# Layer 2's factor products with the weights stationary and 512 tokens moving, and finished tiles turned in 32x32 blocks for the stores

## The chip, the core and the metric

The kernel runs on one core of a Trainium2 chip. The metric is the device time of one execution in microseconds (us). Three runs of the kernel before gave 1584.54, 1584.80 and 1585.04 us; the median is 1584.8 us.

The core's engines are TensorE (PE in the profile, with its weight loads as PEld), VectorE (DVE), ScalarE (ACT), GpSimd (POOL) and SyncE (SP), which here issues nearly all DMAs. They run beside each other and wait for each other by semaphores.

## The reference

Linear attention per batch and head, an RMS norm, and then two feed-forward layers over 4608 tokens (512 wide, 2048 inside), all in float32:

```python
kv = np.einsum('bhsd,bhse->bhde', k, v)
out = np.einsum('bhsd,bhde->bhse', q, kv)
x = out / np.sqrt(np.mean(out * out, -1, keepdims=True) + 1e-6) * g_norm     # -> (4608, 512)
h = x @ w_in1;  x = (h * sigmoid(1.702 * h)) @ w_out1                         # layer 1
h = x @ w_in2;  y = (s * relu(h) ** 2 + b) @ w_out2                           # layer 2, the output
```

## The kernel before

**Numbers.** Every matrix product is made of three matmuls: each operand is split into a high part of reduced precision (fp32r) and a low part, and high x high, low x high and high x low are summed in PSUM.

**Stages.** Attention and the first three blocks of 512 tokens of layer 1 come first. The other six blocks of layer 1 run as three couples of two blocks, and the first eight blocks of layer 2 as four couples. In a couple the input product is made by Strassen-like seven products instead of eight (`product`, three matmuls for each of two 128-row halves, so six matmuls of 128 rows by 512 tokens). The last block of layer 2 is computed plainly (`last_mm1`, `last_mm2`) and is called the tail here.

**Ticks.** One `product` and what stands beside it is a tick; a couple has 8 x 7 = 56 ticks. Layer 2's couples begin at ticks 168, 224, 280 and 336, the tail at tick 392.

**Layer 2's output product.** It is done by seven factor products too. Two pairs of hidden blocks (14 ticks) make a quad. `factor_add` forms the seven sums of activations (names M1, M4, M7, M5, M6, M2, M3 in their order), `factor_hi` and `factor_lo` split each into two tiles `fac`. Factors take two pairs of places by turns: the one the places `wc` and `wo5`, the other `wo6` and `wo7`, so every second factor uses `wc`/`wo5`. `load_t` brings the factors of the weights from DRAM into a ring of five places. In each tick `quad_unit` computes one half (h = 0 or 1) of one factor: with 4 quads in each of 4 couples that is 4 x 4 x 7 x 2 = 224 units. A unit is 12 matmuls (lines 993 to 995): 128 tokens of `fac` are the stationary side, 256 columns of the weights move, and the result has tokens on the partitions. Five of the seven factors are drained by VectorE into an SBUF tile `madd` after each unit, from two PSUM banks taken by turns; M2 and M3 stay in PSUM over the whole couple (`msum`).

**Places in SBUF.** `PLACES` lays all tiles out one behind the other. Six small tiles of 32 bytes (`ms0 r0 ms1 r1 r2 r3`) stand behind `wf0`; all places named after them lie 192 bytes off the 2 KB grid of those named before (`kv`, `f`, `q`, `wraw`, `wst0`, `wc`, `xn`). `wo0` to `wo7`, `wi`, `xh`, `xl` and `wst1` are among the later ones.

**End of a couple.** `combine(s, h)`, once for each h, adds the seven factors on VectorE (line 89 records all VectorE and ScalarE work) and sends four results of 256 tokens x 256 columns each straight from `madd` with one DMA each on SP (line 1018).

**What sets the order.** The program order of each engine is written out: the loop over pairs and products calls `product`, `after`, `factors`, `beside_quads` and then `background`, which steps waiting tasks by release and due ticks. SP takes its DMAs strictly in that order: a DMA that waits for a tile holds all those behind it.

Of the kernel before, what the change touches and what calls it, by code (L numbers as in the profile page):

```python
# [16 lines left out]
P = 128  # L17
# [5 lines left out]
BT = 512  # L23
# [7 lines left out]
PARTS = HEAD + [(ALONE, 0, KF)]  # L31
SIZES = {"kv": 1024, "wraw": 1024, "wst": 1024, "wc": 1024, "wo": 1024, "f": 1024, "xh": 2048, "xl": 2048, "wi": 2048, "ms": H, "r": H}
PLACES = (
# [3 lines left out]
)  # L37
# [3 lines left out]
KP = DM // 2  # L41
# [11 lines left out]
def tile_attn_moe_moe2(  # L53
# [18 lines left out]
    nc = tc.nc  # L72
# [20 lines left out]
    vector = Metered(nc.vector, "dve", 75, 1.04)  # L93
    scalar = Metered(nc.scalar, "act", 95, 0.83)
# [32 lines left out]
    def bank(tag, name, shape=(P, BT)):  # L127
        return ps.tile(list(shape), F32, tag=tag, name=name)
# [550 lines left out]
    g2_t, c_t, ps_t, sums = {}, {}, {}, {}  # L679
# [291 lines left out]
    def held(q_, k_):  # L971
        return k_ in (M2, M3)

    def quad_unit(q_, k_, h):

        s, x = quads[q_]
        first, last = x == 0, x == KF // 2 // BY - 1
        hi, lo, _ = f_t[q_, k_]
        w = t_t[q_, k_]
        key = (s, k_, h)  # L980
        if not held(q_, k_):
            turns["m"] = turns.get("m", -1) + 1
            o = bank(("h1", "a1")[turns["m"] % 2], "m", (P, 2, KP))
        elif first:
            o = m_ps[key] = bank(f"y{len([0 for z in m_ps if z[0] == s])}", "msum", (P, 2, KP))
        else:
            o = m_ps[key]
        for c in range(2):
            cs = slice((2 * h + c) * P, (2 * h + c + 1) * P)
            for y in range(BY):  # L990
                begins = c == 0 and y == 0 and (first or not held(q_, k_))
                ends = c == 1 and y == BY - 1 and (last or not held(q_, k_))
                nc.tensor.matmul(o[:, c, :], hi[:, y, cs], w[:, y, 0, :], start=begins, stop=False)  # L993
                nc.tensor.matmul(o[:, c, :], hi[:, y, cs], w[:, y, 1, :], start=False, stop=False)  # L994
                nc.tensor.matmul(o[:, c, :], lo[:, y, cs], w[:, y, 0, :], start=False, stop=ends)  # L995
        if not held(q_, k_):
            if first:
                a = m_sb[key] = new(ADD_PLACE[10 + h if k_ == M1 and s % 2 else 2 * k_ + h], (P, 2, KP), name="madd")
                scalar.copy(a, o)
            else:  # L1000
                a = m_sb[key]
                vector.tensor_tensor(out=a, in0=o, in1=a, op=ALU.add)
        if last:
            ended.add(key)
        if h == 1:
            load_t()

    ended = set()

    def combine(s, h):  # L1010

        js, m = couples[s][2], couples[s][1]
        q_ = quads.index((s, 0))
# [6 lines left out]
        def plus(k_, more):  # L1020
            a = m_sb[s, k_, h]
            vector.tensor_tensor(out=a, in0=more, in1=a, op=ALU.add)

        def until(k_):
            while (s, k_, h) not in ended:
                yield 1

        sums = ((M7, M6), (M6, M5), (M5, M7), (M7, M4))
        plus(M6, m_sb[s, M1, h])
        if s == LAST - 1:  # L1030
            yield from until(M2)
            plus(M1, m_ps[s, M2, h])
            yield from until(M3)
            last = new(f"f{h}", (P, 2, KP), name="m3")
            scalar.copy(last, m_ps[s, M3, h])
            yield 4
            send(M1, 0, 0)
            for k_, e in sums:
                plus(k_, m_sb[s, e, h])
                yield 2  # L1040
            send(M5, 1, 1)
            plus(M6, last)
            yield 2
            send(M7, 1, 0)
            yield 2
            send(M6, 0, 1)
            return
        yield from until(M6)
        for k_, e in sums:
            plus(k_, m_sb[s, e, h])  # L1050
            yield 1
        send(M5, 1, 1)
        yield from until(M2)
        plus(M1, m_ps[s, M2, h])
        yield 1
        send(M7, 1, 0)
        yield 1
        send(M1, 0, 0)
        yield from until(M3)
        plus(M6, m_ps[s, M3, h])  # L1060
        yield 1
        send(M6, 0, 1)

    wo2_next = [0]

# [48 lines left out]
    n0 = begin[1, CUTS[-2]]  # L1114
# [10 lines left out]
    n0 = begin[ALONE, 0]  # L1125
# [85 lines left out]
    class Task:  # L1211
# [4 lines left out]
        def step(self, tick):  # L1216
            wait = next(self.gen, self)
            if wait is self:
                self.done = True
                tasks.remove(self)  # L1220
            else:
                self.ready = max(self.ready, tick + (wait or 0))

    def plan():

        n = KF // 2 * 7
        split = {}
        for s_ in range(len(couples)):
            n0 = n * s_
            need = []  # L1230
            if s_:
                if couples[s_][0]:
                    need = [Task(y_get(s_), n0 - n + 6, n0 - n + 7)]
                if s_ < LAST:
                    need = [Task(fac_sums(s_), n0 - (14 if s_ <= first2 else 35), n0 - 9, need)]
            for i in range(7 if s_ < LAST else 2):
                if (s_, i) in split_early:
                    continue
                more = [split[s_, 1]] if (i == 6 and s_ <= first2 and (s_, 1) in split) else []
# [19 lines left out]
    with tc.manual_schedule():  # L1259
# [10 lines left out]
        o = bank("h1", "warm")  # L1270
# [399 lines left out]
```

## Time and profile before

| what | value |
|---|---|
| median of three runs | 1584.8 us |
| the profiled execution's own time | 1585.22 us |
| its span, first to last instruction | 1583.5 us |
| TensorE matmuls in it | 8880, busy 99% of the span |
| VectorE, ScalarE busy | 63%, 59% |
| stores of layer 2's couples (line 1018) | 32 DMAs of 256 KB |

A busy TensorE is not TensorE at its peak: the profile's matmuls overlap, so what a matmul costs is read from the start of one to the start of the next, which the timeline shows. The profiled execution's span leaves 1.7 us of its time outside.

### The profile page before, as it was taken

What the parts mean: (1) busy time and instruction counts of PE and PEld (TensorE: products, weight loads), DVE (VectorE), ACT (ScalarE), POOL (GpSimd) and SP (SyncE); (2) the same over time, 40 slices, a digit from 0 to 9 for tenths busy, and PEclk for the clock granted to TensorE, in tenths of its full rate; (3) what the DMA queues carried; (4) which work ended last, traced back from release to release, by engine and by line L of the source; (5) the groups of instructions that cost most, each with busy time, mean ns of one, the idle gap of its engine ahead of it and who ended that gap; (6) DMA issues with size and microseconds to landing.
All of it is one profiled execution on the core that took longest, in us unless ns stands there. A gap on an engine that the chain in (4) does not pass through costs nothing.

```text
span 1583.5 us, 23132 instructions
## 1 busy us (share of the span) xinstructions
PE 1563.4 (99%) x8880; PEld 1338.7 (85%) x8880; DVE 1001.3 (63%) x1478; ACT 937.4 (59%) x1520; POOL 69.3 (4%) x49
## 2 busy tenths in 40 slices
PE   7999999999999999999999999999999999999999
PEld 6788888878887888888888899899999998999987
DVE  6877743456666666777885466866686668556620
ACT  4766643454445555464446866776677677766652
POOL 4000111101000010000000000000000000000000
PEclk9999999999999999999999999999999999999999
DMA  8678877567776876789975755685568556755563
GB/s 279 199 265 308 274 259 258 199 207 244 272 240 231 293 255 219 248 278 362 357 282 199 253 188 186 213 268 189 185 216 263 188 188 210 241 193 184 189 219 113
DMA packets 127039, 372.71 MB, mean 235 GB/s; under 512 B 12626, under 2 KB 29266, under 8 KB 119762
## 3 DMA queue, kind: packets, MB, share of 16 engines
q1 hardware_dynamic: 126786, 371.12, 69.6%
q8 instruction: 70, 1.15, 0.3%
q14 instruction: 39, 0.32, 0.1%
q10 hardware_dynamic: 144, 0.13, 0.0%
HBM read 289.41 MB, written 81.79 MB: 234 GB/s over the span
## 4 chain that ended last, share of the span: by engine, by line
PE 90%; DVE 5%; ACT 2%; DMA 2%; issue 1%; SPq 0%; POOL 0%; DVEq 0%; ACTq 0%; POOLq 0%
PE A L696 6%; PE A L697 6%; PE A L698 6%; PE m L995 4%; PE m L994 4%; PE m L993 4%; PE D L696 3%; PE D L697 3%; PE D L698 3%; PE sum L830 3%; PE sum L832 3%; PE sum L831 3%; PE acc L624 3%; PE acc L625 3%; PE z L830 3%; PE acc L626 3%
## 5 line engine op out<-in xcount | busy, mean ns | idle before, releaser
L995 PE MATMUL m<-wo,fac 128*128 128x256 f32 x640 | 180.8, 283 | 0.6 <-DVE fac L89 0.6
L994 PE MATMUL m<-wo,fac 128*128 128x256 f32 x640 | 180.7, 282 | 0.0
L993 PE MATMUL m<-wo,fac 128*128 128x256 f32 x640 | 180.0, 281 | 0.0
L89 ACT ACTIVATE gh<-gh 128x512 f32<-128x512 f32 x72 | 45.4, 632 | 145.3 <-DVE gh L89 145.2
L994 PEld LDWEIGHTS m<-wo,fac 128*128 128x128 f32 x640 | 122.2, 191 | 6.1
L993 PEld LDWEIGHTS m<-wo,fac 128*128 128x128 f32 x640 | 121.2, 189 | 7.0
L995 PEld LDWEIGHTS m<-wo,fac 128*128 128x128 f32 x640 | 121.2, 189 | 1.2 <-DVE fac L89 1.2
L696 PE MATMUL A<-wi,xl 128*128 128x512 f32 x296 | 117.5, 397 | 1.9 <-ACT ev L89 0.7
L697 PE MATMUL A<-wi,xl 128*128 128x512 f32 x296 | 116.2, 393 | 0.0
L698 PE MATMUL A<-wi,xl 128*128 128x512 f32 x296 | 115.2, 389 | 0.0
L89 DVE TENSOR_TENSOR madd<-m,madd 128x512 f32<-128x512 f32 x122 | 83.8, 688 | 49.4 <-PE m L995 49.4
L89 ACT ACTIVATE wraw<-wraw 128x512 uint32<-128x512 uint32 (+1 forms) x128 | 82.7, 646 | 52.6 <-DVE wraw L89 52.6
L425 POOL TENSOR_TENSOR r<-ms,mhalf 128x8 f32<-128x8 f32 x36 | 65.6, 1826 | 544.0 <-DVE ms L89 543.9
L89 DVE TENSOR_TENSOR fac<-s,fac 128x1024 fp32r<-128x1024 f32 x64 | 77.9, 1218 | 15.0 <-ACT fac L89 15.0
L89 ACT ACTIVATE g<-h 128x512 f32<-128x512 f32 x52 | 31.0, 597 | 79.8 <-PE h L598 69.6
L596 PE MATMUL h<-xh,wi 128*128 128x512 f32 x192 | 76.5, 399 | 1.2 <-ACT g L89 1.2
L830 PE MATMUL z<-wo,wo 128*128 128x512 f32 x192 | 76.1, 396 | 1.2 <-DVE g L89 0.7
L624 PE MATMUL acc<-gh,wo 128*128 128x512 f32 x192 | 76.7, 399 | 0.0
L625 PE MATMUL acc<-gh,wo 128*128 128x512 f32 x192 | 75.1, 391 | 0.7 <-DVE wo L89 0.7
L626 PE MATMUL acc<-gl,wo 128*128 128x512 f32 x192 | 75.0, 390 | 0.0
L598 PE MATMUL h<-xl,wi 128*128 128x512 f32 x192 | 74.9, 390 | 0.0
L832 PE MATMUL z<-wo,wo 128*128 128x512 f32 x192 | 74.9, 390 | 0.0
(264 smaller groups left out, 4370.7 us busy)
## 6 DMA issues: line engine op xcount, KB each, us to landing
wo<-wt SPq DMA_DIRECT2D x127, 512.0 KB, 4.0
wo<-wo SPq DMA_DIRECT2D x80, 512.0 KB, 5.1
xl<-wi SPq DMA_DIRECT2D x37, 1024.0 KB, 6.5
xl<-wi SPq DMA_DIRECT2D x37, 768.0 KB, 5.9
wi<-wst SPq DMA_DIRECT2D x40, 512.0 KB, 4.5
xh<-wi SPq DMA_DIRECT2D x19, 1024.0 KB, 6.7
wraw<-in_w_in SPq DMA_DIRECT2D x32, 512.0 KB, 4.1
wraw<-in_w_out SPq DMA_DIRECT2D x32, 512.0 KB, 4.4
```

Of the source, the lines that this page charges most:

```text
L89: return fn(*args, **kw)
L624: nc.tensor.matmul(o, wh[:, ds_], gh, start=(f == lo), stop=False)
L625: nc.tensor.matmul(o, wl[:, ds_], gh, start=False, stop=False)
L626: nc.tensor.matmul(o, wh[:, ds_], gl, start=False, stop=(f == hi - 1))
L696: nc.tensor.matmul(o, wh, xh, start=(c == 0 and not more), stop=False, skip_group_check=more)
L697: nc.tensor.matmul(o, wl, xh, start=False, stop=False, skip_group_check=more)
L698: nc.tensor.matmul(o, wh, xl, start=False, stop=(c == 1), skip_group_check=more)
L830: nc.tensor.matmul(o, wh[:, cs], gh, start=begins, stop=False)
L832: nc.tensor.matmul(o, wh[:, cs], gl, start=False, stop=ends)
L993: nc.tensor.matmul(o[:, c, :], hi[:, y, cs], w[:, y, 0, :], start=begins, stop=False)
L994: nc.tensor.matmul(o[:, c, :], hi[:, y, cs], w[:, y, 1, :], start=False, stop=False)
L995: nc.tensor.matmul(o[:, c, :], lo[:, y, cs], w[:, y, 0, :], start=False, stop=ends)
```

## The change

The operands of `quad_unit` change sides. The weights' factor (128 x 128) is the stationary side and all 512 tokens of `fac` move, so a unit is 6 matmuls of 512 columns (lines 992 to 994 of the new file), and the result has 128 output columns on the partitions and 512 tokens along the row. h now picks 128 of the 256 columns instead of 256 of the 512 tokens.

The output must have tokens as rows. So `combine`, now one task for both h, lets VectorE transpose each finished 128 x 512 tile in 32 x 32 blocks into one of three places, and four DMAs per tile put the blocks where they belong, in runs of 32 floats (128 bytes). The sums come in another order, and the sends have due ticks of their own (`COMBINE_DUE`, `LAST_DUE`, tables of due ticks counted from the couple's end). A 2 KB place `tr0` is added.

```diff
-    "kv0 kv1 f0 f1 f2 f3 f4 f5 q0 q1 wraw0 wraw1 wst0 wc xn0 xn1 wf0 "
+    "kv0 kv1 f0 f1 f2 f3 f4 f5 q0 q1 wraw0 wraw1 wst0 wc xn0 xn1 wf0 tr0 "
...
-        for c in range(2):
-            cs = slice((2 * h + c) * P, (2 * h + c + 1) * P)
-            for y in range(BY):
-                begins = c == 0 and y == 0 and (first or not held(q_, k_))
-                ends = c == 1 and y == BY - 1 and (last or not held(q_, k_))
-                nc.tensor.matmul(o[:, c, :], hi[:, y, cs], w[:, y, 0, :], start=begins, stop=False)
-                nc.tensor.matmul(o[:, c, :], hi[:, y, cs], w[:, y, 1, :], start=False, stop=False)
-                nc.tensor.matmul(o[:, c, :], lo[:, y, cs], w[:, y, 0, :], start=False, stop=ends)
+        hs = slice(h * P, (h + 1) * P)
+        for y in range(BY):
+            begins = y == 0 and (first or not held(q_, k_))
+            ends = y == BY - 1 and (last or not held(q_, k_))
+            nc.tensor.matmul(o, w[:, y, 0, hs], hi[:, y, :], start=begins, stop=False)
+            nc.tensor.matmul(o, w[:, y, 1, hs], hi[:, y, :], start=False, stop=False)
+            nc.tensor.matmul(o, w[:, y, 0, hs], lo[:, y, :], start=False, stop=ends)
...
-    def combine(s, h):
+    combined = {}
+
+    def combine(s):
+
+        js = couples[s][2]
+        last = s == LAST - 1
-        def send(k_, t, right):
-            row = js[0] * BT + t * m + 2 * h * P
-            dst = out[row:row + 2 * P, right * KP:(right + 1) * KP].rearrange("(c p) d -> p c d", p=P)
-            nc.sync.dma_start(out=dst, in_=m_sb[s, k_, h])
+        def send(k_, t, right, h):
+            row, col = js[t] * BT, (2 * right + h) * P
+            turns["z"] = turns.get("z", -1) + 1
+            z = new(("tr0", "kv0", "kv1")[turns["z"] % 3] if last else ("tr0", "ev0", "g1")[turns["z"] % 3], name="turned")
+            vector.transpose(out=z, in_=m_sb[s, k_, h])
+            dst = out[row:row + BT, col:col + P].rearrange("(b i) (a j) -> a i b j", i=32, j=32)
+            for a in range(P // 32):
+                nc.sync.dma_start(out=dst[a], in_=z[32 * a:32 * a + 32, :].rearrange("i (b j) -> i b j", j=32))
...
+        yield from until(M6)
+        for k_, e in ((M7, M6), (M6, M5), (M5, M7), (M7, M4)):
+            for h in range(2):
+                plus(k_, h, m_sb[s, e, h])
+                yield step()
+        if not last:
+            yield from until(M2)
+            for h in range(2):
+                plus(M1, h, m_ps[s, M2, h])
+                yield step()
+        for h in range(2):
+            send(M7, 1, 0, h)
+            yield step(1)
...
+    COMBINE_DUE = (6, 7, 10, 10, 11, 11, 12, 12, 13, 13, 13, 14, 15, 16, 17, 18, 18, 19, 19, 20, 21, 22, 23)
...
-                for h in range(2):
-                    Task(combine(s_, h), n0 + n + 2 + h, n0 + n + 7 + h)
+                combined[s_] = 0
+                Task(combine(s_), n0 + n + 2, lambda s_=s_, t=n0 + n: t + (LAST_DUE if s_ == LAST - 1 else COMBINE_DUE)[combined[s_]])
```

Where this moves instructions is seen on VectorE and SP behind the end of a couple. VectorE's program order there in the kernel before, from the product B of one pair to the product D; `madd` are the factors' sums, `msum` PSUM, `s1` to `s3` and `fac` the next quad's factors, `wi7`, `xh0`, `wraw` and `wst0` activations:

```order
L89 TENSOR_TENSOR wi7_9549<-B_9576,wi7_9549 128x512
L89 TENSOR_TENSOR fac_9554<-wraw1_9234,fac_9553 128x1024
L89 TENSOR_TENSOR madd_8258<-msum_8353,madd_8258 128x512
L89 TENSOR_TENSOR s1_9614<-wst0_9202,wraw1_9234 128x1024
L89 TENSOR_TENSOR fac_9617<-s3_9551,fac_9616 128x1024
L89 TENSOR_TENSOR wi7_9549<-A_9542,wi7_9549 128x512
L89 TENSOR_TENSOR s2_9673<-s1_9614,wraw0_9138 128x1024
L89 TENSOR_TENSOR xh0_9612<-D_9637,xh0_9612 128x512
```

The same stretch of VectorE's order in the changed kernel, where `turned` is the place that a transposed tile goes to:

```order
L89 TENSOR_TENSOR wi7_9210<-B_9229,wi7_9210 128x512
L89 TENSOR_TENSOR fac_9215<-wraw1_8965,fac_9214 128x1024
L89 STREAM_TRANSPOSE turned_9250<-madd_8086 128x512
L89 TENSOR_TENSOR s1_9264<-wst0_8939,wraw1_8965 128x1024
L89 STREAM_TRANSPOSE turned_9280<-madd_8106 128x512
L89 TENSOR_TENSOR fac_9267<-s3_9212,fac_9266 128x1024
L89 STREAM_TRANSPOSE turned_9306<-madd_8129 128x512
L89 TENSOR_TENSOR wi7_9210<-A_9203,wi7_9210 128x512
L89 TENSOR_TENSOR s2_9322<-s1_9264,wraw0_8887 128x1024
L89 STREAM_TRANSPOSE turned_9336<-madd_8151 128x512
L89 TENSOR_TENSOR xh0_9262<-D_9286,xh0_9262 128x512
```

Of the eight transposes of a couple four stand in this stretch and four behind it, one in each tick from 15 to 22 after the couple's end; before, the last addition of the couple stood here, and no result was sent after tick 16.

SP's program order behind the end of the first couple of layer 2 in the kernel before; `out<-madd` are the stores, `wo<-wt` and `xl<-wi` loads of weights, `f3<-y5` a load of the next couple's input:

```order
L1018 DMA out<-madd_8170 128x2x256
L498 DMA f3_9341<-y5_87 128x2x512
L125 DMA wo2_9535<-wt0_3842 128x1024
L1018 DMA out<-madd_8115 128x2x256
L1018 DMA out<-madd_8198 128x2x256
L125 DMA xl1_9540<-wi1_3_5356 128x2048
L1018 DMA out<-madd_8002 128x2x256
L1018 DMA out<-madd_8141 128x2x256
L125 DMA wo3_9601<-wt0_3842 128x1024
```

And in the changed kernel, where each tile's store is four DMAs `out<-turned` (the `x4` of a row):

```order
L1023 DMA out<-turned_9250 32x16x32 x4
L1023 DMA out<-turned_9280 32x16x32 x4
L125 DMA wo4_9304<-wt0_3843 128x1024
L1023 DMA out<-turned_9306 32x16x32 x4
L125 DMA xl0_9312<-wi1_3_5357 128x1536
L1023 DMA out<-turned_9336 32x16x32 x4
L125 DMA wo0_9362<-wt1_3844 128x1024
L1023 DMA out<-turned_9366 32x16x32 x4
L1023 DMA out<-turned_9393 32x16x32 x4
L125 DMA xh1_9399<-wi1_4_5897 128x2048
```

The stores of a couple are 32 DMAs of 64 KB instead of 8 of 256 KB, they begin three ticks later, and four or eight of them stand ahead of each weight load on the same queue.

## Rows read from the trace of the kernel before

**Rows 1.** The page: engines, granted TensorE clock by slice, the chain that ended last
```profile
PE 1563.4 (99%) x8880; PEld 1338.7 (85%) x8880; DVE 1001.3 (63%) x1478; ACT 937.4 (59%) x1520; POOL 69.3 (4%) x49
...
PEclk9999999999999999999999999999999999999999
...
PE 90%; DVE 5%; ACT 2%; DMA 2%; issue 1%; SPq 0%; POOL 0%; DVEq 0%; ACTq 0%; POOLq 0%
```

**Rows 2.** PE's groups by line and shape: xcount | busy us, mean ns | idle
```profile
L995 PE MATMUL m<-wo,fac 128*128 128x256 f32 x640 | 180.8, 283 | 0.6 <-DVE fac L89 0.6
...
L995 PE MATMUL msum<-wo,fac 128*128 128x256 f32 x256 | 72.2, 282 | 0.0
```

**Rows 3.** Timeline of PE (start us, us): first factor matmul, first matmul after the last
```profile
880.53 0.28 PE L993 MATMUL m<-wo,fac 128*128 128x256 f32 x1
...
1510.00 0.40 PE L892 MATMUL h<-wi,xl 128*128 128x512 f32 x1
```

**Rows 4.** Timeline of PE, a tick with `fac` in `wo6`/`wo7`: unit, product, next unit
```profile
891.77 0.28 PE L993 MATMUL m<-wo,fac 128*128 128x256 f32 x1
...
893.20 0.40 PE L696 MATMUL D<-wi,xl 128*128 128x512 f32 x1
...
894.59 0.28 PE L993 MATMUL m<-wo,fac 128*128 128x256 f32 x1
```

**Rows 5.** Timeline of PE, a tick with `fac` in `wc`/`wo5`: unit, product, next unit
```profile
886.17 0.28 PE L993 MATMUL m<-wo,fac 128*128 128x256 f32 x1
...
887.58 0.40 PE L696 MATMUL D<-wi,xl 128*128 128x512 f32 x1
...
888.97 0.28 PE L993 MATMUL m<-wo,fac 128*128 128x256 f32 x1
```

**Rows 6.** Timeline of PE in layer 1: twelve matmuls of 512 columns
```profile
842.83 0.39 PE L830 MATMUL sum<-wi,wo 128*128 128x512 f32 x1
...
845.55 0.39 PE L696 MATMUL A<-wi,xh 128*128 128x512 f32 x1
```

**Rows 7.** Timeline of PE in the tail: twelve matmuls from `wst0`, then twelve from `wst1`
```profile
1522.53 0.39 PE L917 MATMUL sum<-wo,wst 128*128 128x512 f32 x1
...
1525.32 0.39 PE L917 MATMUL sum<-wo,wst 128*128 128x512 f32 x1
...
1528.11 0.39 PE L917 MATMUL sum<-wo,wst 128*128 128x512 f32 x1
...
1530.83 0.39 PE L917 MATMUL sum<-wo,wst 128*128 128x512 f32 x1
```

**Rows 8.** Waits from 880 to 1511 us: total us, times, longest us
```profile
PEld m L995 <- DVE fac L89: 1.2, 3, 0.4
...
DVE madd L89 <- PE m L995: 49.4, 54, 2.1
```

**Rows 9.** Windows behind a couple's end: length, PE, PEld, DVE, ACT, POOL, clock, DMA share, GB/s
```profile
1043.80:1049.40 5.60, 5.60 (x38) 5.09 (x37) 2.43 (x3) 4.43 (x7) 0.00 (x0) 1.00 1.00 347
...
1055.00:1060.70 5.70, 5.70 (x38) 5.18 (x37) 2.36 (x2) 5.63 (x10) 0.00 (x0) 1.00 0.82 244
1060.70:1066.30 5.60, 5.60 (x38) 5.09 (x37) 5.20 (x6) 5.17 (x9) 0.00 (x0) 1.00 0.38 129
```

**Rows 10.** VectorE's groups by shape: xcount | busy us, mean ns | idle
```profile
L89 DVE TENSOR_TENSOR fac<-s,fac 128x1024 fp32r<-128x1024 f32 x64 | 77.9, 1218 | 15.0 <-ACT fac L89 15.0
...
L89 DVE TENSOR_SCALAR wf<-wf 128x512 f32<-128x512 f32 x64 | 27.0, 422 | 12.4 <-ACT wf L89 12.3
```

**Rows 11.** The stores of line 1018: ns min/median/max on SP, and us to landing
```profile
L1018 SPq DMA_DIRECT2D out<-madd x32: 379/433/1053, 1032.0 to 1555.1; - x32
...
DMA to landing us min/median/max: 4.3/6.1/9.3
```

**Rows 12.** DMA queue from 12.0 to 13.5 us, then 95 to 97 us: packets, MB, share
```profile
q1 hardware_dynamic: 947, 0.44, 101.9%
...
q1 hardware_dynamic: 675, 0.63, 89.7%
```

More of the change, by code (lines that the diff above doesn't have):

```diff
@@ L982, in quad_unit @@
             turns["m"] = turns.get("m", -1) + 1
-            o = bank(("h1", "a1")[turns["m"] % 2], "m", (P, 2, KP))
+            o = bank(("h1", "a1")[turns["m"] % 2], "m")
         elif first:
-            o = m_ps[key] = bank(f"y{len([0 for z in m_ps if z[0] == s])}", "msum", (P, 2, KP))
+            o = m_ps[key] = bank(f"y{len([0 for z in m_ps if z[0] == s])}", "msum")
         else:
             o = m_ps[key]
-        for c in range(2):
-            cs = slice((2 * h + c) * P, (2 * h + c + 1) * P)
-            for y in range(BY):
-                begins = c == 0 and y == 0 and (first or not held(q_, k_))
-                ends = c == 1 and y == BY - 1 and (last or not held(q_, k_))
-                nc.tensor.matmul(o[:, c, :], hi[:, y, cs], w[:, y, 0, :], start=begins, stop=False)
-                nc.tensor.matmul(o[:, c, :], hi[:, y, cs], w[:, y, 1, :], start=False, stop=False)
-                nc.tensor.matmul(o[:, c, :], lo[:, y, cs], w[:, y, 0, :], start=False, stop=ends)
+        hs = slice(h * P, (h + 1) * P)
[5 more added lines that the diff above has]
+            nc.tensor.matmul(o, w[:, y, 0, hs], lo[:, y, :], start=False, stop=ends)
         if not held(q_, k_):
             if first:
-                a = m_sb[key] = new(ADD_PLACE[10 + h if k_ == M1 and s % 2 else 2 * k_ + h], (P, 2, KP), name="madd")
+                a = m_sb[key] = new(ADD_PLACE[10 + h if k_ == M1 and s % 2 else 2 * k_ + h], name="madd")
                 scalar.copy(a, o)
@@ L1008, in tile_attn_moe_moe2, with plus @@
     ended = set()
-    def combine(s, h):
-        js, m = couples[s][2], couples[s][1]
-        q_ = quads.index((s, 0))
-        def send(k_, t, right):
-            row = js[0] * BT + t * m + 2 * h * P
-            dst = out[row:row + 2 * P, right * KP:(right + 1) * KP].rearrange("(c p) d -> p c d", p=P)
-            nc.sync.dma_start(out=dst, in_=m_sb[s, k_, h])
-        def plus(k_, more):
+    combined = {}
[10 more added lines that the diff above has]
+                nc.sync.dma_start(out=dst[a], in_=z[32 * a:32 * a + 32, :].rearrange("i (b j) -> i b j", j=32))
+        def plus(k_, h, more):
             a = m_sb[s, k_, h]
@@ L1024, in until, with step @@
         def until(k_):
-            while (s, k_, h) not in ended:
+            while (s, k_, 1) not in ended:
                 yield 1
-        sums = ((M7, M6), (M6, M5), (M5, M7), (M7, M4))
-        plus(M6, m_sb[s, M1, h])
-        if s == LAST - 1:
+        def step(wait=0):
+            combined[s] += 1
+            return wait
+        m3 = {}
+        for h in range(2):
+            plus(M6, h, m_sb[s, M1, h])
+            yield step()
+        if last:
             yield from until(M2)
-            plus(M1, m_ps[s, M2, h])
+            for h in range(2):
+                plus(M1, h, m_ps[s, M2, h])
+                yield step()
@@ L1033, in combine @@
             yield from until(M3)
[L1034 to L1047, printed above, removed]
-        yield from until(M6)
-        for k_, e in sums:
-            plus(k_, m_sb[s, e, h])
-            yield 1
@@ L1052, in combine @@
[L1052 to L1058, printed above, removed]
-        yield from until(M3)
-        plus(M6, m_ps[s, M3, h])
-        yield 1
-        send(M6, 0, 1)
+            for h in range(2):
+                m3[h] = new(f"f{h}", name="m3")
+                scalar.copy(m3[h], m_ps[s, M3, h])
+                yield step()
+        yield from until(M6)
+        for k_, e in ((M7, M6), (M6, M5), (M5, M7), (M7, M4)):
+            for h in range(2):
+                plus(k_, h, m_sb[s, e, h])
+                yield step()
@@ new lines, in combine @@
+        if not last:
+            yield from until(M2)
+            for h in range(2):
+                plus(M1, h, m_ps[s, M2, h])
+                yield step()
+        for h in range(2):
+            send(M7, 1, 0, h)
+            yield step(1)
+        for h in range(2):
+            send(M5, 1, 1, h)
+            yield step(1)
+        yield from until(M3)
+        for h in range(2):
+            plus(M6, h, m3[h] if last else m_ps[s, M3, h])
+            yield step()
+        for h in range(2):
+            send(M6, 0, 1, h)
+            yield step(1)
@@ L1064, in tile_attn_moe_moe2 @@
+        for h in range(2):
+            send(M1, 0, 0, h)
+            yield step(1)
+    LAST_DUE = (6, 7, 11, 12, 13, 13, 14, 15, 16, 16, 17, 17, 18, 18, 19, 20, 21, 22, 23, 23, 24, 25, 26, 27, 28)
+    COMBINE_DUE = (6, 7, 10, 10, 11, 11, 12, 12, 13, 13, 13, 14, 15, 16, 17, 18, 18, 19, 19, 20, 21, 22, 23)
     wo2_next = [0]
```

## The prediction

> **What bounds the kernel now.** I read the page first: TensorE is busy for 99% of the span at the full granted clock (every slice at 9 tenths or more, the 2.4 GHz level), and 90% of the chain that ended last is TensorE's own matmuls [rows 1]. Next the groups by line: the factor products, which the change rewrites, are 896 matmuls on each of three lines (640 into `m`, 256 into `msum`), 2688 of 256 columns [rows 2]. Then the waits of that stretch: TensorE waited for their operands 3 times, 1.2 us in all [rows 8]. So layer 2 is bound by the rate at which TensorE takes matmuls, and a busy time of 282 ns each says little about it, since they overlap. The rate is read from starts in the timeline.
>
> From the first factor matmul to the first matmul after the last one are 1510.00 - 880.53 = 629.5 us [rows 3], for 224 units with a product after each but the last. A tick, unit and product, takes 894.59 - 891.77 = 2.82 us where the factor lies in `wo6`/`wo7` [rows 4] and 888.97 - 886.17 = 2.80 us where it lies in `wc`/`wo5` [rows 5]; 112 x 2.82 + 112 x 2.80 = 629.4 us, so these two rows explain the whole stretch. Within the ticks a unit's 12 matmuls take 1.43 or 1.41 us (119 and 118 ns each) and the product's 6 of 512 columns 1.39 us (232 ns each).
>
> **Part 1: six matmuls of 512 columns for twelve of 256.** Columns in all stay the same; what goes is a fixed cost per matmul. In layer 1, where nothing but 512-column matmuls stand one behind the other, twelve take 845.55 - 842.83 = 2.72 us, 226.7 ns each [rows 6], less than two of 256 columns (2 x 119 = 238 ns). The product's own matmuls run at 232 ns only in layer 2, behind 256-column ones, so they gain as well: a tick could become 12 such matmuls, 2.72 us.
>
> Whether it does depends on where the operands lie. In the tail, too, all matmuls have 512 columns, yet the twelve of unit and product take 1525.32 - 1522.53 = 2.79 us with the stationary tile in `wst0`, and 1530.83 - 1528.11 = 2.72 us with it in `wst1` [rows 7]. By the list of places `wst1` lies on the same 192-byte offset as the moving weights and `wst0` doesn't. After the change units with `wo6`/`wo7` have all operands on one offset: 2.72 us, a gain of 0.10 x 112 = 11.2 us. Units with `wc`/`wo5` have a moving tile on the other offset in 4 of 6 matmuls; the tail had the stationary one there, so no row shows this case. Its ends are 2.72 and 2.79 us, gains of 9.0 and 1.1 us; both rows are equally near, so I take the middle, 5.0 us. Sum of part 1: -16.2 us (-12.3 to -20.2).
>
> The Trainium skill, page "TensorE: Matmul & The Clock Gate", section "Wait — 56ns, not 53.3ns?", gives a matmul at full clock N/2.4 ns plus a fixed 2.5 ns or so. By it, an estimate, 1344 matmuls fewer would save only 1344 x 2.5 ns = 3.4 us. The trace disagrees: two of 256 columns cost 11 ns more than one of 512 [rows 4, 6].
>
> **Part 2: the waits that are there.** The three waits of a weight load for a split factor [rows 8] come at a couple's start, where ScalarE and VectorE run behind for about five ticks. TensorE gains 0.05 to 0.10 us per tick on them, some 0.35 us, so each grows by that: +1.1 us (0 to 1.5). The time that VectorE waited for `m` is 49.4 us in the same stretch [rows 8], which is its reserve elsewhere.
>
> **Part 3: the transposes.** 32 of 128 x 512. No row shows one; the nearest are 0.42 us (an operation of this size in a fast form) and 1.22 us (one of twice the size) [rows 10]. I take 0.7 us, 22 us in all. They stand in ticks 15 to 22 behind a couple's end, where VectorE is busy 2.43 of 5.60 and 2.36 of 5.70 us [rows 9]: one per tick adds 1.4 us to such a slice and fits. Only the slice behind, 5.20 of 5.60, would overflow by up to 1 us. The additions are the same in number. Cost 0.
>
> **Part 4: the stores.** Each tile goes out as 4 DMAs, 2048 packets of 128 bytes, 128 for each of 16 DMA engines. Packets of 465 bytes on average took 1.019 x 16 x 1500 / 947 = 25.8 ns, those of 933 bytes 0.897 x 16 x 2000 / 675 = 42.5 ns [rows 12]. The line through both gives 13.8 ns at 128 bytes; by bytes alone it would be 7 ns, and at most the 42.5 ns of the packet that is replaced. I take 14 ns: 1.8 us per tile, beside loads that need about 0.60 of a tick (the mean of the shares 0.82 and 0.38 [rows 9]), 1.6 us: 3.4 us of DMA work in a tick of 2.72 us, for eight ticks.
>
> This counts because a transpose may only start when the tile three before has left its place, 3 x 2.72 = 8.2 us later. From transpose to landing are 0.7 + 4 x 0.43 (four issues) + 6.1 us [rows 11] = 8.5 us, plus 0.7 us more for each tile queued. So VectorE will wait, 0.3 us and then up to 4 us in the last tiles of a couple, and behind the waiting transpose stand the split of the next factor and the drain of `m`. TensorE has two banks for `m`, and can run about 4 us on. I put 1 us on each of three couples; the fourth couple sends in the tail, where the product runs seven steps behind its factors and the end comes some 25 us after the last store of before (1555.1 of 1583.5 us [rows 11]). SP's loads wait behind the stores by up to 2 ticks, with a ring of five places, so eight ticks, in hand. Cost +3 us; the ends are 0 and, with the slowest landing of 9.3 us and a queue on top, 5 us a couple, 15 us.
>
> **Sum.** -16.2 + 1.1 + 3.0 = -12.1 us on the profiled execution's 1585.2 us: 1573.1 us. That execution lay 0.4 us above the median of the runs, so 1572.7 us.
>
> **The rivals.**
> - *All clean.* Both kinds of unit run at 2.72 us and the stores hide: 1584.8 - 20.2 + 1.1 = 1565.7 us. For it: layer 1's rows; against it: 7 of 8 of the tail's units are on the slow side. Chance 0.23.
> - *The rate doesn't come.* The 512-column matmuls keep the 232 ns that they have in this stretch [rows 4, 5]: a tick of 2.78 us, gains of 0.04 and 0.02 us, 112 x 0.06 = 6.7 us, of which parts 2 and 4 take 4.1: 1582.2 us, no change that can be told. For it: `wc` units disturb every second pair of ticks; against it: after one change of tile the tail's matmuls were clean at once [rows 7]. Chance 0.10.
> - *The stores take it back.* VectorE stands at a transpose for a place whose four DMAs haven't landed, in ticks 18 to 22 of a couple, and TensorE behind it. With p ns per packet a tick's DMA work is 0.128 p + 1.6 us; what exceeds 2.72 us adds up over five tiles. At 25.8 ns that is 2.2 x 5 + 0.3 - 4 = 7.3 us a couple, 22 us in three: 1572.7 - 3 + 22 = 1591.7 us, slower. At 42.5 ns it is 4.3 x 5 + 0.3 - 4 = 18 us a couple, some 1623 us. The gain is gone at 5 us a couple, from 22 ns a packet on. For it: DMA is already at 1.00 in one slice of this stretch [rows 9]; against it: the line of rows 12. Chance 0.17.
>
> The Trainium skill, page "DMA: Bandwidth & Descriptors", section "Specifications", says that below 512 bytes the DMA engine reads, modifies and writes. By that rule 128-byte stores would be no cheaper than 512-byte ones, which is this last rival; no run here shows such a store yet.
>
> **How the numbers follow.** A measurement of this kernel can tell about 0.2%, 3.2 us. The forecast, 1567 to 1580 us, has chance 0.46; all clean 0.23; no rate 0.10 (0.04 of it still faster); the stores 0.17 (0.12 slower, 0.03 same, 0.02 faster); 0.04 is left for what I don't see, mostly on the slow side. Faster 0.46 + 0.23 + 0.04 + 0.02 = 0.75, same 0.06 + 0.03 = 0.09 and 0.01 of the rest, 0.10; slower 0.15. The range that holds 8 in 10 runs from all clean with no cost at the stores and waits, about 1563 us, to 1590 us, where most of the stores' rival begins.
>
> **What would show it.** Right: units of six matmuls with starts 226.7 ns apart where `fac` is in `wo6`/`wo7`, ticks of 2.72 us there, and 2.72 to 2.79 us at the others; 32 transposes near 0.7 us; TensorE's waits in the stretch under 8 us, those that are new at transposes' successors. The stretch of 629.5 us becomes about 617 us. Wrong: ticks of 2.78 us everywhere (part 1), or VectorE idle before transposes for a DMA `out<-turned` by more than 5 us a couple, with TensorE waiting for VectorE behind it (part 4).

## The result and the profile after

The changed kernel takes 1570.65 us (median of four runs, 1570.61 to 1572.51) against 1584.92 us of the kernel before: a ratio of 0.9910, 95% interval 0.9893 to 0.9927. The forecast was 1572.7 us. The profiled execution of the changed kernel is the longest of its four, 1572.51 us; the other three agree within 0.05 us and have spans of 1568.8 to 1568.9 us in place of 1570.7. The difference lies ahead of the stretch in question, which begins at 882.17 us in it, and at 879.9 to 880.7 us in four of the runs below whose code ahead of it is the same.

The page: the same columns in 1344 matmuls fewer; the chain is still TensorE's [rows 1].

```profile
PE 1550.3 (99%) x7536; PEld 1272.0 (81%) x7536; DVE 1021.4 (65%) x1510; ACT 936.1 (60%) x1520; POOL 69.3 (4%) x49
...
PE 89%; DVE 5%; ACT 3%; DMA 2%; issue 1%; SPq 0%; POOL 0%; ACTq 0%; DVEq 0%; POOLq 0%
```

The timeline of TensorE (start us, us), the first factor matmul and the first matmul after the last one: 1497.29 - 882.17 = 615.12 us, where before it was 629.47 [rows 3]. That is 14.35 us, the whole gain.

```profile
882.17 0.39 PE L992 MATMUL m<-fac,wo 128*128 128x512 f32 x1
...
1497.29 0.39 PE L892 MATMUL h<-wi,xl 128*128 128x512 f32 x1
```

The same view, a unit, its product and the next unit with `fac` in `wo6`/`wo7`: 1.36 + 1.36 = 2.72 us in place of 2.82 [rows 4].

```profile
893.13 0.39 PE L992 MATMUL m<-fac,wo 128*128 128x512 f32 x1
...
894.49 0.39 PE L696 MATMUL D<-wi,xl 128*128 128x512 f32 x1
...
895.85 0.39 PE L992 MATMUL m<-fac,wo 128*128 128x512 f32 x1
```

And with `fac` in `wc`/`wo5`: 1.40 + 1.36 = 2.76 us in place of 2.80 [rows 5]. Of its matmuls the two in three that move the high part, which lies in `wc`, take 0.235 to 0.237 us to the next start (medians), the third, which moves `wo5`, 0.228 us.

```profile
887.61 0.40 PE L992 MATMUL m<-fac,wo 128*128 128x512 f32 x1
...
889.01 0.39 PE L696 MATMUL D<-wi,xl 128*128 128x512 f32 x1
...
890.37 0.40 PE L992 MATMUL m<-fac,wo 128*128 128x512 f32 x1
```

The waits from 880 to 1511 us (total us, times, longest us) [rows 8]. TensorE now waits a little more, at each couple's start: 2.3 us for `fac` in place of 1.2, and 1.1 us for `wst`, a wait that is new there (the other 1.1 us of that row end at 880.7 us, ahead of the stretch, where the kernel before waited as well). VectorE waits 3.7 us for stores, and TensorE waits nowhere where the transposes stand (1041 to 1062 us for the first couple).

```profile
DVE madd L89 <- PE m L994: 45.7, 56, 2.0
...
DVE turned L89 <- DMA out<-turned: 3.7, 5, 1.0
...
PEld m L994 <- DVE fac L89: 2.3, 3, 0.8
PEld A L696 <- ACT wst L89: 2.2, 4, 1.1
```

The new tile `turned`: the stores' ns on SP and the transposes' (min/median/max), then the stores' us from issue to landing.

```profile
L1023 SPq DMA_DIRECT2D out<-turned x128: 337/506/2579, 1042.0 to 1542.6; - x128
L89 DVE STREAM_TRANSPOSE turned<-madd x32: 669/705/712, 1041.3 to 1536.4; 128x512 f32<-128x512 f32 x32
...
DMA to landing us min/median/max: 2.0/3.8/6.5
```

### The profile page after: what moved, and what is told of

Same layout as the page of the kernel before. It is cut to its first block, busy times and chain, and to the rows that moved or that the text cites. A ratio compares the mean times of both kernels' runs of the same rounds, so it can differ in the third digit from the quotient of the medians.

```text
span 1570.7 us, 20568 instructions
## 1 busy us (share of the span) xinstructions
PE 1550.3 (99%) x7536; PEld 1272.0 (81%) x7536; DVE 1021.4 (65%) x1510; ACT 936.1 (60%) x1520; POOL 69.3 (4%) x49
## 4 chain that ended last, share of the span: by engine, by line
PE 89%; DVE 5%; ACT 3%; DMA 2%; issue 1%; SPq 0%; POOL 0%; ACTq 0%; DVEq 0%; POOLq 0%
PE A L696 6%; PE A L697 6%; PE A L698 6%; PE m L994 4%; PE m L993 4%; PE m L992 4%; PE D L696 3%; PE D L697 3%; PE D L698 3%; PE z L830 3%; PE sum L830 3%; PE sum L832 3%; PE sum L831 3%; PE z L832 3%; PE z L831 3%; PE acc L624 3%
## 5 line engine op out<-in xcount | busy, mean ns | idle before, releaser
L994 PE MATMUL m<-fac,wo 128*128 128x512 f32 x320 | 125.2, 391 | 1.1 <-DVE fac L89 1.1
L992 PE MATMUL m<-fac,wo 128*128 128x512 f32 x320 | 125.8, 393 | 0.0
L993 PE MATMUL m<-fac,wo 128*128 128x512 f32 x320 | 125.7, 393 | 0.0
L596 PE MATMUL h<-xh,wi 128*128 128x512 f32 x192 | 76.5, 398 | 1.2 <-ACT g L89 1.2
L830 PE MATMUL z<-wo,wo 128*128 128x512 f32 x192 | 76.1, 396 | 1.2 <-DVE g L89 0.7
L832 PE MATMUL z<-wo,wo 128*128 128x512 f32 x192 | 74.8, 390 | 0.0
L831 PE MATMUL z<-wo,wo 128*128 128x512 f32 x192 | 74.8, 389 | 0.0
L597 PE MATMUL h<-xh,wi 128*128 128x512 f32 x192 | 74.8, 389 | 0.0
L994 PEld LDWEIGHTS m<-fac,wo 128*128 128x128 f32 x320 | 59.9, 187 | 16.2 <-DVE fac L89 2.3
```

The lines of the kernel that those rows point to most:

```text
L596: nc.tensor.matmul(o, wh[:, cs], xh[:, c, :], start=(c == 0), stop=False)
L830: nc.tensor.matmul(o, wh[:, cs], gh, start=begins, stop=False)
L831: nc.tensor.matmul(o, wl[:, cs], gh, start=False, stop=False)
L832: nc.tensor.matmul(o, wh[:, cs], gl, start=False, stop=ends)
L992: nc.tensor.matmul(o, w[:, y, 0, hs], hi[:, y, :], start=begins, stop=False)
L993: nc.tensor.matmul(o, w[:, y, 1, hs], hi[:, y, :], start=False, stop=False)
```

## The experiments

Twelve kernels, in the order in which they ran.

**All places on one grid.** Is the slow unit slow by its address?

```diff
-    "ms0 r0 ms1 r1 r2 r3 xh0 xl0 ...
+    "xh0 xl0 ...
-    "... wi4 wi5 wi6 wi7"
+    "... wi4 wi5 wi6 wi7 ms0 r0 ms1 r1 r2 r3"
```

> The changed kernel with the six small tiles of 32 bytes named last in the list of places, so that all other places lie on one 2 KB grid. Theory (offset): a matmul is slower when its moving tile, or its stationary one, lies 192 bytes off the grid of the other operand. Then the 112 units with `wc`/`wo5` go from 1.40 us to 1.36 us (112 x 0.04 = 4.5 us) and the tail's 384 matmuls from 229 to 232 ns to 226.7 ns (1.5 us): 1570.6 - 6.0 = 1564.6 us. Rival (the place or its neighbours' traffic is slow, whatever the offset): the units keep 1.40 us, 1570.6 us.

Measured: 1564.79 us, ratio 0.9875 (0.9858 to 0.9891). The timeline of a unit in `wc`/`wo5`, its product and the next unit reads 1.36 and 1.36 us; the tail's matmuls stand 226 to 227 ns apart. The forecast was met by 0.2 us, so the address is the cause and the place is not. This is the fastest form of all that ran.

```profile
885.44 0.39 PE L992 MATMUL m<-fac,wo 128*128 128x512 f32 x1
...
886.80 0.39 PE L696 MATMUL D<-wi,xl 128*128 128x512 f32 x1
...
888.16 0.39 PE L992 MATMUL m<-fac,wo 128*128 128x512 f32 x1
```

**Streams alone.** The same question without any other engine.

```diff
+    for n, so, mo in STREAMS:                  # columns, shifts in words of 4 bytes
+        ...
+            w = st[:, so + 128 * (c % 4):so + 128 * (c % 4) + 128]
+            x = mv[:, mo + 512 * (c % 2):mo + 512 * (c % 2) + n]
+            nc.tensor.matmul(o[:, 0:n], w, x, start=(c == 0), stop=(c == 11))
```

> Only streams of matmuls, 48 or more of each kind, with no other engine at work; nothing of the reference is computed and the output is constant. Stationary and moving tile are shifted by 0, 32, 64, 96, 128, 192, 256, 384, 512 or 1024 bytes against each other. Theory (offset): 226.7 ns from start to start at equal offsets, 232 to 237 ns at 192 bytes of difference on either side, and at 64 bytes too if what counts is the address within 128 bytes. 256 columns: about 119 ns, 128 columns about 65 ns, a fixed cost of 12 to 13 ns per matmul. Rival (traffic of other engines makes the difference): 226.7 ns at every offset, and 256 columns at half of that, 113 ns.

The timeline, one row per stream (start us, us from the first start to the last end, count). In order: 512 columns with the moving tile 192 bytes off, on the grid, and both tiles 96 bytes off; 256 columns on the grid, and with the moving tile 192 bytes off.

```profile
76.86 11.36 PE L95 MATMUL n512s0m<-mv,st 128*128 128x512 f32 x48
...
131.93 11.05 PE L95 MATMUL n512s0m<-mv,st 128*128 128x512 f32 x48
...
231.54 10.61 PE L95 MATMUL n512s24m<-mv,st 128*128 128x512 f32 x46
...
286.57 11.44 PE L95 MATMUL n256s0m<-mv,st 128*128 128x256 f32 x94
297.97 10.95 PE L95 MATMUL n256s0m<-mv,st 128*128 128x256 f32 x95
```

Less one matmul's own 0.39 us and divided by the count less one, these are 233.4, 226.8 and 227.1 ns; with 0.28 us for 256 columns 120.0 and 113.5 ns (113.3 by the starts alone, without the first matmuls). Of all shifts tried, 512 columns took 226.7 ns where both tiles were shifted alike, or against each other by 256, 512 or 1024 bytes, and 229 to 234 ns at 32, 64, 96, 128, 192 and 384 bytes. So an effect of the address needs no other engine, and with 512 columns it follows the difference of the two addresses. What I had not expected: 256 columns go the other way. With the moving or the stationary tile 192 bytes off, or the stationary one 64 bytes, they cost half of 512 columns, with no fixed cost left; with the moving tile 64 bytes off they took 117.8 ns in the same run. 128 columns took 111.7 ns, not the 65 ns expected: under 256 columns the time hardly falls.

**The halves of 256 columns.** Is it the number of matmuls or their sides?

```diff
-        for y in range(BY):
-            nc.tensor.matmul(o, w[:, y, 0, hs], hi[:, y, :], ...)
+        for c in range(2):
+            cs = slice(c * KP, (c + 1) * KP)
+            for y in range(BY):
+                nc.tensor.matmul(o[:, cs], w[:, y, 0, hs], hi[:, y, cs], ...)
```

> The changed kernel with each factor matmul made in two halves of 256 moving columns, 12 per unit as before, the weights still stationary. Theory (the number of matmuls): the unit takes 1.42 to 1.43 us again and the products behind it 1.39 us, ticks of 2.80 to 2.82 us, so the whole gain of the matmuls goes: 1570.6 + 15 = 1585 us or so. Rival (which operand is stationary makes the gain, for instance since the weights' tile is loaded where `fac` was): units of 1.36 to 1.40 us, within 2 us of 1570.6 us.

Measured: 1585.99 us, ratio 1.0008 (0.9998 to 1.0017). The timeline of TensorE: unit 1.43 us, tick 889.80 - 886.99 = 2.81 us. All of the gain goes, with the weights still stationary: the width of the matmuls makes it. Their number goes with the width, and so does that of the weight loads, one for each matmul (8880 and 7536 of either on the two pages), so no run here tells these apart. TensorE's weight loads wait 1.1 us for `fac` in this run, near the 1.2 us of the kernel before.

```profile
886.99 0.40 PE L696 MATMUL D<-wi,xl 128*128 128x512 f32 x1
...
888.37 0.28 PE L994 MATMUL m<-fac,wo 128*128 128x256 f32 x1
...
889.80 0.40 PE L696 MATMUL A<-wi,xl 128*128 128x512 f32 x1
```

**The kernel before on one grid** (the edit of the first experiment). 

> The kernel before with the six small tiles named last, so that all other places lie on one 2 KB grid. Theory (offset): units with `wc`/`wo5` take the 1.432 us of those with `wo6`/`wo7` in place of 1.413 us (112 x 0.02 = 2.2 us longer) and the tail gains 1.5 us: 1584.9 + 0.7 = 1585.6 us. Rival (offset worth as much as with 512 columns): units gain 0.02 to 0.04 us, 1579 to 1581 us. Rival (the place, not the offset): 1584.9 us.

Measured: 1584.69 us, ratio 1.0002 (0.9992 to 1.0011). The units in `wc`/`wo5` went to 1.43 us, as the theory had it; their median is 1.433 us and the stretch grew from 629.5 to 631.5 us. So the grid alone costs 256 columns 2.0 us; the tail, with its matmuls of 512 columns, is 1.5 us shorter (1583.7 - 1511.76 us in place of 1583.5 - 1510.00), and in all it comes to nothing.

```profile
885.87 0.28 PE L993 MATMUL m<-wo,fac 128*128 128x256 f32 x1
...
887.30 0.40 PE L696 MATMUL D<-wi,xl 128*128 128x512 f32 x1
```

**No transposes, plain stores.**

```diff
-            vector.transpose(out=z, in_=m_sb[s, k_, h])
-            ...
-            for a in range(P // 32):
-                nc.sync.dma_start(out=dst[a], in_=z[32 * a:32 * a + 32, :]...)
+            row += col
+            nc.sync.dma_start(out=out[row:row + P, :], in_=m_sb[s, k_, h])
```

> The changed kernel without the 32 transposes, each tile stored by one DMA of 128 packets of 2 KB; the output keeps features as rows within each block, which isn't the reference's. It prices transposes and 128-byte stores together. Theory (they are hidden: packets of 128 bytes took 13 ns in the changed kernel and a store lands in 3.8 us): within 0.5 us of the changed kernel's 1570.6 us. Rival (the step of the prediction that put 3 us on them): 1567.6 us.

Measured: 1571.37 us (1569.85 to 1572.96), ratio 0.9912 (0.9898 to 0.9927), the same as the changed kernel's. The stretch, by the timeline, is 1495.87 - 880.71 = 615.16 us against 615.12. Transposes and 128-byte stores cost nothing that can be measured.

```profile
880.71 0.39 PE L992 MATMUL m<-fac,wo 128*128 128x512 f32 x1
...
1495.87 0.39 PE L892 MATMUL h<-wi,xl 128*128 128x512 f32 x1
```

**One place for the transposed tiles.** When would the stores decide?

```diff
-            z = new(("tr0", "kv0", "kv1")[turns["z"] % 3] if last else ("tr0", "ev0", "g1")[turns["z"] % 3], name="turned")
+            z = new("tr0", name="turned")
```

> The changed kernel with one place in place of three for the transposed tiles, so each transpose waits for the four stores of the one before. From transpose to landing are about 0.7 + 0.5 x 4 issues in part beside the transfer + 3.8 = 6.2 us, against ticks of 2.72 us. Theory (VectorE's wait reaches TensorE after the some 4 us that its two PSUM banks allow): 7 waits of 3.5 us less 4 us are 20 us a couple, 60 us in three couples, and a few in the tail: 1630 us or so. Rival (VectorE's reserve takes it): under 1580 us.

Measured: 1620.25 us, ratio 1.0222 (1.0205 to 1.0239): the theory's mechanism, which is that of the prediction's rival on the stores, at some five sixths of the price I gave it. Three transposes in VectorE's timeline (idle before and its releaser at the end):

```profile
1044.91 0.71 DVE L89 STREAM_TRANSPOSE turned<-madd 128x512 f32<-128x512 f32 x1 [4.09 <-DMA out<-turned]
...
1049.21 0.71 DVE L89 STREAM_TRANSPOSE turned<-madd 128x512 f32<-128x512 f32 x1 [2.48 <-DMA out<-turned]
...
1053.49 0.71 DVE L89 STREAM_TRANSPOSE turned<-madd 128x512 f32<-128x512 f32 x1 [1.86 <-DMA out<-turned]
```

One directly behind the other they follow at 4.3 us: that is transpose, four issues and landing. And TensorE's timeline a little later:

```profile
1075.93 0.80 PE L994 MATMUL msum<-fac,wo 128*128 128x512 f32 x1 [4.98 <-DVE fac L89]
1076.52 0.63 PE L992 MATMUL msum<-fac,wo 128*128 128x512 f32 x1
1076.95 0.63 PE L993 MATMUL msum<-fac,wo 128*128 128x512 f32 x1
```

It waited 4.98 us for a split that stood behind such a transpose, and then took 427 ns a matmul. In the windows of that run the granted clock was 0.50 of full speed from 1076 to 1080 us, the level of 1.2 GHz, and 1.00, that of 2.4 GHz, from 1081 us on. So a long wait can be paid a second time in a slow clock behind it: in five such places 47 matmuls stood 427 ns apart in place of 227, some 9 us of the 50 that one place costs.

**Two places.** The place is chosen by `turns["z"] % 2` from `tr0` and `ev0` (`kv0` for the last couple). 

> The changed kernel with two places in place of three for the transposed tiles. Two ticks are 5.44 us and a transpose with its stores about 6.2 us. Theory (waits add up and reach TensorE beyond 4 us): 6 waits of 0.8 us less 4 us, about 1 us a couple: 1570 to 1575 us, with VectorE's waits for the stores well over the 9 us of the changed kernel. Rival (the chain is as long as the 8.5 us of the prediction): 6 x 3.1 - 4 = 15 us a couple, some 1615 us.

Measured: 1575.22 us (1573.14 to 1577.18), ratio 0.9936 (0.9922 to 0.9951): just above the first theory's range, and far from the rival's 1615 us. By the waits of the stretch VectorE stood 21.3 us for stores, and TensorE began to wait for `fac` behind a couple's end: starts over 0.3 us apart lose 4.9 us in the stretch, against 2.5 us with three places. Three places are enough, and two are not.

```profile
DVE turned L89 <- DMA out<-turned: 21.3, 9, 3.1
...
PEld m L994 <- DVE fac L89: 3.0, 5, 0.8
...
PEld msum L994 <- DVE fac L89: 2.2, 3, 1.0
```

**Factors off the grid, before and after.** If 256 columns run best off the grid, the kernel before should gain by it, and the changed one lose.

```diff
-    "ms0 r0 ms1 r1 r2 r3 xh0 ...
-    "... wo4 wo5 wo6 wo7 wi4 ...
+    "wo5 wo6 wo7 ms0 r0 ms1 r1 r2 r3 xh0 ...
+    "... wo4 wi4 ...
```

> The kernel before, with `wo5`, `wo6` and `wo7` named ahead of the six small tiles, so that both tiles of every factor lie 192 bytes off the moving weights' grid; still twelve matmuls of 256 columns a unit and the plain stores. Theory (address): the streams alone gave 113.3 ns for 256 columns at that difference and 120.0 ns without one, so a unit of twelve takes 1.36 to 1.39 us and its product 1.36 to 1.39 us; the stretch of 629.5 us becomes 609 to 623 us, and layer 1, where `wo5` is one of six places of weights, loses 1 to 2 us: 1573 us or so (1566 to 1581). Rival (the prediction's term: a fixed cost of 12 to 13 ns for each matmul, whatever the addresses): units keep 1.41 to 1.43 us, 1584.9 us or more.

Measured: 1588.84 us, ratio 1.0023 (1.0013 to 1.0032). All units take the same time now, but 893.34 - 891.92 = 1.42 us, not 1.36, by the timeline. Here my theory failed and the rival held: the stretch gained 2.2 us only (627.3 us), and layer 1 lost 6 us ahead of it. The expectation had counted `wo5` alone in layer 1, but `wo6` and `wo7` hold moving tiles of its output product (`z<-wo,wo`), whose 576 matmuls stand some 4 ns further apart in this form, 2.3 us of the six.

```profile
891.92 0.28 PE L993 MATMUL m<-wo,fac 128*128 128x256 f32 x1
...
893.34 0.40 PE L696 MATMUL D<-wi,xl 128*128 128x512 f32 x1
```

> The changed kernel with the same three places named ahead of the six small tiles, so that every factor's moving tiles lie 192 bytes off the stationary weights. Theory (address): with 512 columns the shift costs what it gives with 256; all units take the 233 ns a matmul of the streams at that difference, 1.40 us: 112 x 0.04 = 4.5 us more, and 1 to 2 us in layer 1: 1576 to 1577 us. Rival (the place `wc` is slow for another reason): units with `wo6`/`wo7` stay at 1.36 us, 1571 to 1573 us.

Measured: 1583.89 us, ratio 0.9995 (0.9986 to 1.0004), 13 us slower than without the shift. Units with `wo6`/`wo7` rose to 1.384 us (medians), and the products, whose own operands stayed on one grid, to 1.389 us, so the stretch took 621.6 us; layer 1 lost another 6 us, of which I had expected 1 or 2. The direction was right and the size wrong: the products behind such units are slower too. The sign was wrong as well: 233 ns are the streams' figure for a moving tile 192 bytes on, and here, by the list of places, it is the stationary one that lies 192 bytes on, for which they gave 228.9 ns, 1.37 us a unit. The 1.40 us of the `wc` units, with the same sign, isn't that figure either. So the streams show that the address counts, and don't give its price in the kernel.

**Units and products by turns, alone.** Why 118 ns in the kernel, when the stream had 113?

```diff
+                w = st[:, so + 128 * (c % 4):so + 128 * (c % 4) + 128]
+                x = mv[:, mo + n * (c % 2):mo + n * (c % 2) + n]
+                nc.tensor.matmul(o[:, 0:n], w, x, start=(c == 0), stop=(c == 12 * 256 // n - 1))
```

> Only streams of matmuls, no other engine at work; nothing of the reference is computed and the output is constant. Units (12 matmuls of 256 columns, or 6 of 512) stand by turns with products (6 of 512 columns, operands on one grid), as in layer 2, with the unit's moving or stationary tile on the grid or 192 bytes off it. Theory (the turns between two kinds of matmul cost the units of 256 columns what the streams alone didn't show): on the grid 1.43 us a unit and 1.39 us a product, 192 bytes off it 1.41 and 1.39 us, as in the kernel before and its shifted form; six of 512 columns on the grid 1.36 and 1.36 us. Rival (in the kernel the other engines' traffic at SBUF adds it): 113.3 ns for each matmul of a 256-column unit off the grid, 1.36 us, also here.

The timeline: products and units with 256 columns on the grid (`a`), with the moving tile 192 bytes off it (`b`), and 256 columns so shifted without products between (`g`).

```profile
66.96 1.55 PE L96 MATMUL prod_a<-mv,st 128*128 128x512 f32 x6
68.35 1.60 PE L91 MATMUL unit_a<-mv,st 128*128 128x256 f32 x12
69.78 1.55 PE L96 MATMUL prod_a<-mv,st 128*128 128x512 f32 x6
...
123.34 1.52 PE L96 MATMUL prod_b<-mv,st 128*128 128x512 f32 x6
124.70 1.58 PE L91 MATMUL unit_b<-mv,st 128*128 128x256 f32 x12
126.12 0.39 PE L96 MATMUL prod_b<-mv,st 128*128 128x512 f32 x1
...
397.78 13.94 PE L103 MATMUL alone_g<-mv,st 128*128 128x256 f32 x117
```

By medians the unit takes 1.43 and the product 1.39 us on the grid, 1.41 and 1.36 with the moving tile off it, 1.41 and 1.37 with the stationary one off it. Six of 512 columns and their product take 1.36 and 1.36 us on the grid, 1.40 and 1.38 with the moving tile off it, 1.37 and 1.36 with the stationary one. The unit's times are the kernel's, so no traffic of other engines is needed for them (the product behind a shifted unit, 1.36 us, is faster than the 1.39 us of the kernel). But `g` takes (13.94 - 0.28) / 116 = 117.8 ns without any turns: the turns are not the cause either. It differs from the stream of 113.5 ns in that its two moving slices lie 1 KB apart, as the kernel's do, and not 2 KB. But 2 KB alone doesn't do it: with the moving tile 128 or 256 bytes off, such streams took 118.7 and 120.0 ns here. Which distances give 113 ns, and why, stays open.

**The waits at a couple's start.** On the form with one grid, the splits of the next couple's inputs one tick earlier, and one later (with `+ (s_ > first2)` in the same place):

```diff
-                split[s_, i] = Task(split_x(s_, i), ..., max(0, n0 + i - (4 if i < 6 else 5)), need + more)
+                split[s_, i] = Task(split_x(s_, i), ..., max(0, n0 + i - (4 if i < 6 else 5) - (s_ > first2)), need + more)
```

> The aligned form, with the splits of the next couple's inputs (`wi<-f`, at a couple's start on VectorE ahead of the low part of a factor) due one tick earlier in layer 2. In the aligned form TensorE loses 2.9 us in the stretch, in three places of a couple's start, each time waiting for `fac`. Theory (VectorE runs behind there by less than one such split): moved ahead, the waits shrink from about 0.96 us a couple to under 0.4 us, 1.5 to 2.5 us in all: 1562.5 to 1563.3 us. Rival (VectorE's work of these ticks is too much wherever the splits stand): 2.5 us or more stay, 1564.8 us.

Measured: 1574.02 us, ratio 0.9929 (0.9916 to 0.9941): slower than the form it started from. The waits of the stretch: the wait for `fac` is gone, but the splits now stand in pairs ahead of the operations that drain the products' PSUM banks (on ScalarE `xh<-A` comes behind two of them), and the new couple's first product waits 2.4 us for its bank; behind one of these waits matmuls again stood 427 ns apart. Neither theory had that wait.

```profile
PEld A L696 <- ACT xh L89: 7.4, 3, 2.5
...
PE A L696 <- ACT xh L89: 6.1, 3, 2.0
...
PEld A L696 <- ACT wst L89: 1.5, 3, 0.5
```

> The aligned form, with the same splits due one tick later in layer 2. Theory (VectorE runs behind by less than one such split): the low part of `fac` comes out ahead of a split and the waits shrink as well, to 1 to 2 us, if the splits are still in time for their products: 1563 to 1564.5 us. Rival (the splits then come too late for their products): TensorE waits for `wi` instead, 1565 to 1570 us.

Measured: 1565.34 us, ratio 0.9878 (0.9863 to 0.9893), no change against 1564.79. Matmuls that start over 0.3 us after the one before lose 2.9 us in the stretch in both forms, only at other places. So moving a split doesn't help; in the form on one grid VectorE's timeline has no idle time from 995.1 to 1012.5 us, the ticks in question, and its work there is what would have to shrink.

## Why the prediction was right, and where its sizes were off

**Part 1, the matmuls.** Forecast -16.2 us. By ticks it was 112 x (2.82 - 2.72) + 112 x (2.80 - 2.76) = -15.7 us. The middle between the two tail rows for the `wc` units, 5.0 us, became 4.5 us. No row had shown this case, and that the middle came so close is luck: the unit took the tail's slow rate (1.40 us, where half of 2.79 is 1.395), the product behind it the clean one (1.36), and the two together make the middle. That the products behind the units would be clean again, which one rival denied, held at once. The step's reason held for this kernel and not beyond it: two matmuls of 256 columns cost 13 ns more than one of 512 where their operands lie on one grid (2 x 120.0 - 226.7), 9 ns where the factor lies off it as in the shifted form (2 x 118), and nothing in the stream of 113.3 ns. It is no constant of the engine. The Trainium skill, page "TensorE: Matmul & The Clock Gate", section "Wait — 56ns, not 53.3ns?", has N/2.4 ns plus a fixed 2.5 ns or so: for 512 columns that would be 216 ns, an estimate; no stream of 512 columns here went below 226.7 ns.

**Part 2, the waits that are there.** Forecast +1.1 us. TensorE's losses, read from starts over 0.3 us apart, grew from 1.1 us (1.2 us of waits in [rows 8]) to 2.5 us: +1.4 us. The mechanism was right for the waits that were there: the weight loads' waits for `fac` rose from 1.2 to 2.3 us, as forecast, and they are 1.1 us again where the halves of 256 columns slow TensorE down. In the form on one grid, where TensorE is faster still, all losses are 2.9 us. The rest of the 1.4 us is the wait for `wst`, three times some 0.4 us, which the forecast didn't have.

**Part 3, the transposes.** 0.70 us each, as taken; cost nothing, as taken.

**Part 4, the stores, the term that was mis-sized.** Forecast +3.0 us, measured 0 (plain stores changed nothing). The packets were right: 13 ns each (median of the packets' records) where 14 was taken. The chain from transpose to landing, 8.5 us in the forecast, was near the mark as a whole, though not in its parts: a store of 64 KB landed after 3.8 us, where the 6.1 us of one of 256 KB had been taken [rows 11], but the stores stood in SP's queue, and an issue took 0.51 us and not 0.43. VectorE's timeline shows it in the first couple. The seventh transpose takes the place of the fourth and waits for its stores; it begins 1057.22 - 1049.50 = 7.7 us after it.

```profile
1049.50 0.70 DVE L89 STREAM_TRANSPOSE turned<-madd 128x512 f32<-128x512 f32 x1
...
1057.22 0.71 DVE L89 STREAM_TRANSPOSE turned<-madd 128x512 f32<-128x512 f32 x1 [0.91 <-DMA out<-turned]
...
1061.12 0.71 DVE L89 STREAM_TRANSPOSE turned<-madd 128x512 f32<-128x512 f32 x1 [0.56 <-DMA out<-turned]
```

So VectorE waited where the forecast had it, at a couple's last transposes, but 0.5 to 1.7 us a couple and not up to 4. The step that failed is the next one, the 1 us that each of three couples was to cost: waits of this size stay below the some 4 us that TensorE can run on by the forecast's own estimate, and TensorE waited nowhere there. The DMA engines' work was less than forecast, too: they were busy for 0.94 of the time from 1041.0 to 1070.9 us, 2.6 us a tick, where 3.4 had been taken. The two runs with fewer places show what it costs when such waits do reach TensorE: at two places the kernel is 4.6 us slower, at one 50.

The terms with what they measured: -15.7 + 1.4 + 0 = -14.3 us, and the medians differ by 14.27 us. The forecast of -12.1 us was 2.2 us short: 3.0 us by part 4, of which parts 1 and 2 took 0.8 back.

**The rivals.** All clean came at 1564.8 us only with the places on one grid, 0.9 us from the 1565.7 us worked out for it. The rate did come. The stores' rival was real as a mechanism, but its price per packet wasn't: the Trainium skill, page "DMA: Bandwidth & Descriptors", section "Specifications", would have a 128-byte store cost no less than a 512-byte one. The trace doesn't show that price: by the packets' records (medians) 13 ns for 128 bytes, 27 ns for 512 and 46 ns for 1024.

## What to carry to other kernels

Where TensorE is the bound, read the distance from one matmul's start to the next and compare it with a stretch that runs clean; a busy share of 99% hid 20 us here. When a stream of matmuls is a few per cent slow without any wait, compare where its two operands lie, and try to put all tiles on one grid: here one line that moves six small tiles gave 6 us to the changed kernel and nothing to the one before it, so it pays to try it again after the shape of the matmuls has changed. Take the landing of a store from one of the same bytes, count places by transpose, wait in the queue, issues and landing together, and charge a wait of VectorE only where it outlasts what TensorE can run on.

## What the runs showed of the hardware that was not expected

- Addresses: 512 columns take 226.7 ns if moving and stationary tile lie alike, or 256, 512 or 1024 bytes apart, and 229 to 234 ns at the other differences tried. 256 columns take 120.0 ns if they lie alike and 113.3 ns at 192 bytes with moving slices 2 KB apart (117.8 ns with slices 1 KB apart).
- The difference has a sign: with 512 columns the moving tile 64 bytes on or the stationary one 192 bytes on gave 228.9 ns each, and the moving one 192 or the stationary one 64 bytes on 233.3 to 233.4 ns, as if the addresses counted modulo 256 bytes (128 bytes on either side gave 233.5 and 232.4 ns, which fits less well). For 256 columns this doesn't hold: the moving tile 64 bytes on gave 117.8 ns, the stationary one 192 bytes on 113.3.
- 128 columns take 111.7 ns a matmul, nearly as long as 256.
- After a wait of 4.98 us matmuls stood 427 ns apart, at a granted clock of 0.50 (the 1.2 GHz level) from 1076 to 1080 us and 1.00 from 1081 us on.
